# First chunk of a fused attention and feed-forward kernel: softmax sums from a column of ones in v, products scaled per row and transposed back, early buffers in place of late w_out weights

## The chip, the core and the metric

The kernel runs on one core of a Trainium2 chip. The core has a matrix engine (TensorE, PE in the profile; its loads of the stationary operand are PEld), three elementwise engines (VectorE or DVE, ScalarE or ACT, GpSimd or POOL), and a queue, SyncE or SP, that issues all transfers. Each engine works its own queue in order and waits on semaphores for the others. The metric is the device time of one execution in microseconds: the median of three runs was 625.05 us (624.15 to 625.32).

## What is computed

Attention over local windows and block summaries, then a two-layer feed-forward network. There are 4 batches, 8 heads, 768 positions, head size 64, model width 512 and hidden width 2048; all is float32.

```python
k_sum = k.reshape(B, H, nb, block, D).max(axis=3)      # 24 blocks of 32
v_sum = v.reshape(B, H, nb, block, D).mean(axis=3)
scores_l = scale * np.matmul(q, k.transpose(0, 1, 3, 2))
mask_l = np.abs(pos[:, None] - pos[None, :]) < window  # 16
scores_s = scale * np.einsum('bhsd,bhnd->bhsn', q, k_sum) + np.log(block)
scores_all = np.concatenate([np.where(mask_l, scores_l, -1e9), scores_s], axis=-1)
scores_all = scores_all - np.max(scores_all, axis=-1, keepdims=True)
a = np.exp(scores_all)
a = a / (np.sum(a, axis=-1, keepdims=True) + 1e-09)
x = np.matmul(a, np.concatenate([v, v_sum], axis=2))   # then tokens x 512
h = x @ w_in
return np.maximum(0.01 * h, h) @ w_out
```

## The kernel before

**Chunks and units.** The work is cut into 8 chunks (c) of 384 positions. Attention of a chunk runs in 12 units (u, UPC), one for each of four head pairs (p) and three tiles of 128 positions. A unit compares 64 queries at a time with 120 keys: 24 block maxima and 96 positions of a window. The output x of a unit is stored transposed (model width on the partitions) as a high part xh in the matrix engine's fp32r format and the rest xl, so that a product in float32 is three fp32r products. The feed-forward network takes a chunk through 16 hidden tiles (f): `m1` makes a hidden tile with 12 matmuls (L712), ScalarE and VectorE apply the leaky ramp and split it (L716, L719, L722), and `m2` adds its 9 products (L731 to L733) to three accumulators. Later chunks use a Strassen-like scheme (L899, L989), which the change does not touch.

**A unit of chunk 0** (`unit`, L389) goes through these steps, each an entry in the planner's list: `qk`, the scores (L359); `ttr`, mask and row minimum of the negated scores, one operation per head (`lowest`, L364); `ex`, the exponential with the row sum read from ScalarE's accumulator (`expo`, L371); `guard`, `rec` and `nrm`, which add 1e-9, invert the sum and multiply the exponentials by it (L408, L412, L416); `tr`, two transposes (L376); `pt`, a copy of these to SBUF (L427); `av`, four products with v as the stationary operand, which give x already transposed (L382); `xhi` (L433) and `xlo` (L436). Chunk 1 runs in pairs of units, chunks 2 to 7 in fours, between the feed-forward tiles of earlier chunks.

**What a unit needs.** The tile `k` holds q (loaded) and the keys of each tile of positions, copied from the k load `kn` by ScalarE (`windows`, L304, two per head pair) and from the block maxima `ksum` by VectorE (L237, L319). The tile `v` holds the v windows (loaded) and the block means. For batch 0 the means come from TensorE: `v_mean_pe` multiplies three loads `vb` with a small matrix (L273), ScalarE copies the result to `vs` (L278), and GpSimd spreads it into the four v tiles (L315). There are two buffers for k, three for v, two for pt and two for the exponentials e.

**Weights** come as 64-bit loads of 0.52 MB, one for each f and each of w_in (w = 0) and w_out (w = 1), into slots of `big`; VectorE, ScalarE, VectorE, ScalarE, VectorE (L668, L672, L675, L678, L681) turn each into a high and a low tile. The tiles of all 16 f of w_out, `wout_hi` and `wout_lo`, have their own space from the start.

**What sets the order.** A planner (`Plan`) takes all steps with an estimated cost, a priority and their dependences, and writes each engine's queue in the order in which it would run them. Priorities come from `PLACE` (the place of a unit in the stream, by chunk), `OFF` (a shift and a slope for each step of chunk 0 and 1) and a dozen constants (L50 to L64). `LOADS` fixes the order of the first transfers. The planner also decides how many matmuls on zeros (`spare`, L1092) TensorE runs where it expects nothing to do before the feed-forward part begins. What an engine really does at a time is in the trace alone.

## Time and profile before

| | |
|---|---|
| median of three runs | 625.05 us |
| the profiled execution | 625.08 us |
| its span in the trace | 623.3 us |
| TensorE busy | 616.4 us in 4496 matmuls |
| VectorE, ScalarE, GpSimd busy | 367.1, 321.5, 4.4 us |
| transfers | 102.16 MB, 164 GB/s over the span |
| granted clock of TensorE | 0.998 |

The span is the time from the first to the last recorded event; the execution is 1.8 us longer. In the rows that follow, L and a number is the line of the kernel, `out<-in` are the tiles, and the bracket at a row's end tells how long the engine had been idle before it and what ended that. In a table of stretches the columns are: start and end, length, then busy us and (in brackets) instructions of TensorE, its weight loads, VectorE, ScalarE and GpSimd, then the granted clock, the share of the transfer engines in use and GB/s. In a timeline they are start, duration, engine, line, operation and tiles. Matmuls overlap, so the distance from one start to the next tells more than a duration.

### The profile page before, as it was taken

The page shows a single profiled execution, that of the slowest core. Times are in us where ns is not written, and L with a number is a line of the kernel's source. Part 1 is how long each engine was busy: PE and PEld are TensorE (multiplying, and loading weights), DVE is VectorE, ACT ScalarE, POOL GpSimd, SP SyncE. Part 2 cuts the span into 40 slices and gives each one's busy share as a digit, 9 for nine tenths or more (in the row PEclk, how much of TensorE's full clock was granted, in tenths as well). Part 3 has the DMA queues.
Part 4 walks back from the last instruction along what each step waited for, and adds up shares of the span by engine and source line. Part 5 has one row for each costly group of instructions (what it writes and reads, how often), then busy time and mean ns, then how long its engine had stood idle before and what let it go on. Part 6 is the DMA issues. An engine that isn't in the chain of part 4 may idle for free.

```text
span 623.3 us, 12015 instructions
## 1 busy us (share of the span) xinstructions
PE 616.4 (99%) x4496; PEld 541.1 (87%) x4496; DVE 367.1 (59%) x1055; ACT 321.5 (52%) x914; POOL 4.4 (1%) x10
## 2 busy tenths in 40 slices
PE   9999999999999999999999999999999999999996
PEld 7687889888888888888898898989889898989895
DVE  5889999964899433445424763546446751535352
ACT  5889995644776255555525664535435351404040
POOL 0200000000000000000000000000000000000000
PEclk9999999999999999999999999999999999999999
DMA  8897996992787521374231471725416361616122
GB/s 284 249 298 243 291 289 202 367 306 93 227 270 245 144 75 51 90 222 111 83 113 52 124 238 56 221 84 149 124 60 195 118 202 36 202 35 202 38 66 101
DMA packets 58443, 102.16 MB, mean 164 GB/s; under 512 B 5584, under 2 KB 30224, under 8 KB 58384
## 3 DMA queue, kind: packets, MB, share of 16 engines
q1 hardware_dynamic: 58384, 101.38, 52.2%
q8 instruction: 36, 0.59, 0.4%
q14 instruction: 23, 0.19, 0.1%
HBM read 78.33 MB, written 20.97 MB: 159 GB/s over the span
## 4 chain that ended last, share of the span: by engine, by line
PE 94%; ACT 2%; DMA 2%; DVE 1%; issue 0%; DVEq 0%
PE L L989 21%; PE h L712 20%; PE a L731 7%; PE a L733 7%; PE a L732 7%; PE Z L899 5%; PE W L899 5%; PE X L899 5%; PE Y L899 3%; PE spare L1092 2%; DMA big<-in_w_dram 2%; PE vps L273 1%; ACT e L371 1%; PE s L359 0%; PE t L376 0%; ACT big L672 0%
## 5 line engine op out<-in xcount | busy, mean ns | idle before, releaser
L712 PE MATMUL h<-x,win_hi 128*128 128x384 f32 x512 | 131.8, 338 | 0.0
L712 PEld LDWEIGHTS h<-x,win_hi 128*128 128x128 f32 x512 | 92.7, 188 | 4.1
L712 PE MATMUL h<-x,win_lo 128*128 128x384 f32 x256 | 86.1, 336 | 0.0
L722 DVE TENSOR_TENSOR glo<-gs,ghi 128x384 fp32r<-128x384 f32 x64 | 35.5, 555 | 77.4 <-ACT gs L716 77.3
L731 PE MATMUL a<-wout_hi,ghi 128*128 128x512 f32 x192 | 77.4, 403 | 0.2 <-ACT wout_hi L678 0.2
L732 PE MATMUL a<-wout_lo,ghi 128*128 128x512 f32 x192 | 75.2, 392 | 0.5 <-DVE wout_lo L681 0.5
L733 PE MATMUL a<-wout_hi,glo 128*128 128x512 f32 x192 | 75.6, 394 | 0.0
L371 ACT ACTIVATE e<-e,m 128x120 f32<-128x120 f32 x192 | 73.5, 388 | 3.4 <-DVE m L364 3.2
L989 PE MATMUL L<-wout_hi,win_hi 128*128 128x512 f32 x192 | 75.2, 392 | 0.0
L989 PE MATMUL L<-wout_hi,win_lo 128*128 128x512 f32 x192 | 74.9, 390 | 0.0
L989 PE MATMUL L<-wout_lo,win_hi 128*128 128x512 f32 x192 | 74.8, 390 | 0.0
L719 ACT ACTIVATE ghi<-h 128x384 fp32r<-128x384 f32 x64 | 31.4, 491 | 82.9 <-PE h L712 82.4
L712 PEld LDWEIGHTS h<-x,win_lo 128*128 128x128 f32 x256 | 48.0, 188 | 0.0
L733 PEld LDWEIGHTS a<-wout_hi,glo 128*128 128x128 f32 x192 | 36.0, 188 | 8.5 <-DVE glo L722 0.4
L989 PEld LDWEIGHTS L<-wout_hi,win_lo 128*128 128x128 f32 x192 | 36.0, 188 | 7.7
L989 PEld LDWEIGHTS L<-wout_hi,win_hi 128*128 128x128 f32 x192 | 36.0, 188 | 7.0
L989 PEld LDWEIGHTS L<-wout_lo,win_hi 128*128 128x128 f32 x192 | 36.1, 188 | 7.0
L732 PEld LDWEIGHTS a<-wout_lo,ghi 128*128 128x128 f32 x192 | 36.1, 188 | 6.6 <-DVE wout_lo L681 1.2
L731 PEld LDWEIGHTS a<-wout_hi,ghi 128*128 128x128 f32 x192 | 36.1, 188 | 5.9 <-ACT wout_hi L678 0.5
L371 ACT ACTIVATION_READ_ACCUMULATOR e<-e,m 128x1 f32 x192 | 36.9, 192 | 0.0
L940 ACT ACTIVATE win_hi<-U 128x384 fp32r<-128x384 f32 x32 | 16.6, 518 | 38.8 <-DVE U L929 38.8
L955 ACT COPY P<-X 128x384 f32<-128x384 f32 x16 | 7.5, 470 | 50.8 <-PE X L899 49.5
(487 smaller groups left out, 1164.7 us busy)
## 6 DMA issues: line engine op xcount, KB each, us to landing
x<-sums SPq DMA_DIRECT2D x84, 256.0 KB
big<-in_w_dram SPq DMA_DIRECT2D x32, 512.0 KB
v<-in_v_dram SPq DMA_DIRECT2D x32, 288.0 KB
sums<-big SPq DMA_DIRECT2D x16, 512.0 KB
big<-in_k_dram SPq DMA_DIRECT2D x16, 400.0 KB
k<-in_q_dram SPq DMA_DIRECT2D x32, 192.0 KB
big<-in_vb_dram SPq DMA_DIRECT2D x12, 384.0 KB
win_hi<-sums SPq DMA_DIRECT2D x14, 256.0 KB
```

The costliest lines, as they stand in the source:

```text
L371: nc.scalar.activation(out=e[:, n], in_=e[:, n], func=AF.Exp, scale=-1.0, bias=m[:, n:n + 1], accum_out=z[:, n:n + 1])
L712: nc.tensor.matmul(h[:, :T], w[:, 512 * f + 128 * k:512 * f + 128 * k + 128], x[:, T * k:T * k + T], start=n == 0, stop=n == 11)
L719: nc.scalar.activation(out=gnew(tag, G("ghi", f)), in_=tl[G("h", f)][:, :T], func=AF.Prelu, alpha=0.01)
L722: nc.vector.tensor_tensor(out=gnew(tag, G("glo", f)), in0=tl[G("gs", f)], in1=tl[G("ghi", f)].bitcast(F32), op=ALU.subtract)
L731: nc.tensor.matmul(o, gh, wout_hi[:, f], start=f == f0, stop=False)
L732: nc.tensor.matmul(o, gh, wout_lo[:, f], start=False, stop=False)
L733: nc.tensor.matmul(o, gl, wout_hi[:, f], start=False, stop=f == f1 - 1)
L899: nc.tensor.matmul(o[:, :T], w[:, 256 * l + 128 * k:256 * l + 128 * k + 128], x[y][:, T * k:T * k + T], start=start and n == 0, stop=n == ...
L940: nc.scalar.activation(out=hi, in_=ps("X") if direct else tl[kt], func=AF.Prelu, alpha=0.01)
L955: nc.scalar.copy(tmp(K("P1")), ps("X"))
L989: nc.tensor.matmul(o, g, w[:, f], start=s + m == 0, stop=s == 1 and m == 5)
L1092: nc.tensor.matmul(spare[:, :128], zero[:, :128], zero[:, :128], start=True, stop=True)
```

## The change

For chunk 0 alone the exponentials are no longer normalised before they are transposed. The v tiles get 130 columns instead of 128: a column of ones ahead of the first head's and behind the second head's 64, loaded from a new input `v1`, and a further row of 1e-9 in those columns, against a row of ones in `pt`. The value product now has `pt` as the stationary operand and v with its column of ones as the moving one, so it gives 65 columns a head: x by rows, and the sum with its guard beside it. VectorE inverts the two sums (`rec`), scales x by rows (`scale`), TensorE transposes it back into the same bank (`back`), and `xhi` and `xlo` read that. The exponential no longer reads the accumulator, and the guard and the normalisation of e are gone. GpSimd fills the rows and columns of v and pt once at the start.

The last 6 of the 16 w_out tiles get buffers of their own (`late0`, `late1`). Until these are written, the same space (`attic`) holds further buffers of chunk 0: two more for k (q), one for v, four for pt, one for e, so that chunk 0 has four, four, six and three. The product's bank is chosen from two, or four after `HO`.

The planner's numbers change: its estimate of a transfer's latency and rate, some costs, `PLACE`, `OFF`, `LOADS`, and the constants, and the weights' steps are entered after the units.

```diff
-PLACE = {0: (0.0, 1.0), 1: (13.07, 0.61), 2: (22.42, 0.495), 3: (33, 0.8), 4: (43.2, 0.6), 5: (50.4, 0.7)}
+PLACE = {0: (0.015, 0.9806), 1: (13.192, 0.6413), 2: (22.504, 0.3532), 3: (32.642, 0.7357), 4: (43.127, 0.6174), 5: (50.638, 0.7154), 6: (59.023, 0.9778), 7: (71.251, 1.0473)}
...
-    LAT = {"SP": 910.0, "PE": 200.0, "DVE": 130.0, "ACT": 142.0, "POOL": 190.0,
+    LAT = {"SP": 60.0, "PE": 200.0, "DVE": 130.0, "ACT": 142.0, "POOL": 190.0,
...
-    def op(self, eng, cost, prio, fn, after=(), use=(), alloc=(), size=0, rate=250.0, port=False):
+    def op(self, eng, cost, prio, fn, after=(), use=(), alloc=(), size=0, rate=335.0, port=False):
...
-                dma = max(dma, end + 1200) + o["size"] / o["rate"]
+                dma = max(dma, end + 1500) + o["size"] / o["rate"]
...
+    attic = [cst.tile([128, (NF - SPL) * DM], F32, name=f"attic{n}", tag=f"late{n}") for n in range(2)]
...
+    room = {("k", 0, 2): (0, 0), ("k", 0, 3): (0, 1104), ("pt", 2): (0, 2208), ("v", 0, 3): (1, 0), ("pt", 3): (1, 784), ("pt", 4): (1, 1296), ("pt", 5): (1, 1808), ("e", 2): (1, 2320)}
...
+    for p in range(NP):
+        x = first_new("v", ("v", 0, p), [LK + 1, 2 * TPC, 130], VR)
+        nc.gpsimd.memset(x[96:], 0.0)
+        nc.gpsimd.memset(x[96:, :, 0:130:129], 1.0e-9)
+        nc.gpsimd.memset(x[:NS, :, 0:130:129], 1.0)
...
+            nc.gpsimd.memset(tl["pt", m][96:], 1.0)
...
-        def guard():
-            z = tiles_of(m)[2][:, part]
-            nc.vector.tensor_scalar(out=z, in0=z, scalar1=1e-9, scalar2=None, op0=ALU.add)
...
+        def soft(h):
+            e, x, _ = tiles_of(m)
+            n = 2 * (u % 2) + h
+            nc.scalar.activation(out=e[:, n], in_=e[:, n], func=AF.Exp, scale=-1.0, bias=x[:, n:n + 1])
...
         def av():
-            values(u, new(tag_o, ko, [128, 512], src=src_o, bufs=1), 0)
+            o = bank(ko)
+            for j in range(2):
+                for h in range(2):
+                    nc.tensor.matmul(o[64 * j:64 * j + 64, 65 * h:65 * h + 65], tl["pt", m][:, 2 * (u % 2) + h, 64 * j:64 * j + 64],
+                                     tl[kv][:, 2 * i + j, 65 * h:65 * h + 65], start=True, stop=True)
+
+        def rec():
+            nc.vector.reciprocal(out=new("rz", K("rz"), [128, 2]), in_=tl[ko][:, 0:130:129])
...
+        def back():
+            nc.tensor.transpose(out=tl[ko][:, 256:384], in_=tl[K("xr")], identity=ident)
 
         def xhi():
-            nc.scalar.copy(x_of(xh, c, r, 128), tl[ko][:, :128])
+            nc.scalar.copy(x_of(xh, c, r, 128), tl[ko][:, 256:384])
...
+        o = P.op("PE", 200, v + 2.05 + off("back"), back, after=[o], use=[ko, K("xr")])
...
-        o = P.op("ACT", ACT(512), t + 0.3, s4, after=[o], use=[kr])
+        o = P.op("ACT", ACT(512), t + 0.3, s4, after=[o] + ([x for k in room for x in P.users[k]] if w and f >= SPL else []), use=[kr])
...
+    P.settle("o", lambda t: ("a1", "to", "h0", "h1") if t > HO else ("a1", "to"))
```

**How the queues move.** SyncE's queue, from its first transfer, before (in_v_dram into big are the `vb` loads, 128x800 from in_k_dram the `kn` loads):

```order
L233 DMA big<-in_k_dram 128x800
L299 DMA k_1_101<-in_q_dram 128x384
L299 DMA k_0_103<-in_q_dram 128x384
L233 DMA big<-in_k_dram 128x800
L219 DMA mask<-in_mask_dram 128x404
L267 DMA big<-in_v_dram 128x1024
L233 DMA big<-in_k_dram 128x800
L267 DMA big<-in_v_dram 128x1024
L299 DMA k_2_232<-in_q_dram 128x384
L267 DMA big<-in_v_dram 128x1024
L233 DMA big<-in_k_dram 128x800
L660 DMA big<-in_w_dram 128x1024
```

And now, to the same weight load:

```order
L333 DMA k_0_125<-in_q_dram 128x384
L267 DMA big<-in_k_dram 128x800 x2
L333 DMA k_1_129<-in_q_dram 128x384
L253 DMA mask<-in_mask_dram 128x404
L301 DMA big<-in_v_dram 128x1024
L267 DMA big<-in_k_dram 128x800
L333 DMA attic_77<-in_q_dram 128x384
L301 DMA big<-in_v_dram 128x1024 x2
L344 DMA v_0_97<-in_v_dram 96x780
L267 DMA big<-in_k_dram 128x800
L333 DMA attic_77<-in_q_dram 128x384
L700 DMA big<-in_w_dram 128x1024
```

The third and fourth q loads go into space of their own (attic) and stand earlier, and the first v load stands ahead of the fourth kn load.

ScalarE's queue around the copy of the block means (`vs`) and around the twelfth x, before (L304 copies windows, L371 is the exponential, L427 pt, L433 x, L672 and L678 weights):

```order
L371 ACTIVATE e_355,z_357<-e_355,m_356 128x120 x4
L672 ACTIVATE big<-big 128x512
L278 COPY vs_398<-vps 24x512
L678 CAST win_hi<-big 128x512
L433 CAST x_80<-o_434 128x128
...
L433 CAST x_80<-o_639 128x128
L678 CAST wout_hi<-big 128x512
L433 CAST x_80<-o_663 128x128
L672 ACTIVATE big<-big 128x512
L371 ACTIVATE e_673,z_675<-e_673,m_674 128x120 x4
```

And now (L338 windows, L448 and L410 exponentials of chunk 0 and 1, L456 pt, L476 x, L712 weights):

```order
L448 ACTIVATE e_298<-e_298,m_299 128x120 x4
L456 COPY pt_114<-t_314 120x256
L338 COPY attic_77<-big 128x3x96 x2
L312 COPY vs_332<-vps 24x512
L456 COPY pt_114<-t_334 120x256
...
L712 ACTIVATE big<-big 128x512
L476 CAST x_82<-o_539 128x128
L476 CAST x_82<-o_546 128x128
L410 ACTIVATE e_535,z_537<-e_535,m_536 128x120 x2
L476 CAST x_82<-o_567 128x128
L712 ACTIVATE big<-big 128x512
L476 CAST x_82<-o_581 128x128
```

The windows of the fourth head pair stand right ahead of the copy of the means, and exponentials of chunk 1 (`m` 6) and two rescalings of weights stand among the last four x.

TensorE's queue where the feed-forward part begins (L712, now L752), before:

```order
L712 MATMUL h_0_618<-x_80,win_lo 128x384
L382 MATMUL o_639<-pt_631,v_3_467 64x64 x4
L376 MATMUL t_645<-ident,e_542 120x128 x2
L359 MATMUL s_('g', 6, 1)_649<-k_0_379 64x120 x2
L359 MATMUL s_('g', 6, 1)_650<-k_0_379 64x120 x2
L359 MATMUL s_('g', 6, 1)_649<-k_0_379 64x120 x2
L359 MATMUL s_('g', 6, 1)_650<-k_0_379 64x120 x2
L382 MATMUL o_663<-pt_631,v_3_467 64x64 x4
```

And now (L462 is the value product, L473 the transpose back):

```order
L415 MATMUL t_555<-ident,e_437 120x128 x2
L462 MATMUL o_567<-attic_78 64x65 x4
L473 MATMUL o_539<-ident,xr_564 128x128
L473 MATMUL o_546<-ident,xr_572 128x128
L462 MATMUL o_581<-attic_78 64x65 x4
...
L473 MATMUL o_567<-ident,xr_590 128x128
L473 MATMUL o_581<-ident,xr_600 128x128
L752 MATMUL h_0_608<-x_82,win_hi 128x384
L752 MATMUL h_0_608<-x_86,win_hi 128x384
L752 MATMUL h_0_608<-x_82,win_lo 128x384
```

Before, nine matmuls of the first hidden tile stood ahead of the last two value products and the scores of chunk 1; now all products and transposes of chunk 0 and these scores stand ahead of the first of them. Over the whole queue the spares fall from 164 to 53.

More of the change, by code (lines that the diff above doesn't have):

```diff
@@ L456, in unit @@
+        o2 = P.op("DVE", DVE(128), v + 2.2 + off("xlo"), xlo, after=[o1], use=[ko, ("x", c)])
         x_op.setdefault(c, []).extend([o1, o2])
@@ L987, in block @@
                         gh, gl = (y[:, 128 * i:128 * i + 128] for y in g_of(f, h))
[L988 to L989 removed]
+                        for g, w in ((gh, 0), (gh, 1), (gl, 0)):
+                            nc.tensor.matmul(o, g, wout(w, f), start=s + m == 0, stop=s == 1 and m == 5)
                             m += 1
@@ L1044, in build @@
         quad(q)
+    for f in range(NF):
+        for w in range(2):
+            weights(f, w, LEAD - WT + min(f, SPL) * WS + max(f - SPL, 0) * WS2 + WO * w + (W0 if f == 0 else 0))
     t = LEAD
```

161 lines of the change are left out of this document (86 added, 75 removed).

## Prediction

> **What bounds the kernel now.** I read the page's busy shares first, then the table by stretches, then the timeline of the first 35 us, engine by engine.
>
> ```profile
> PE 616.4 (99%) x4496; PEld 541.1 (87%) x4496; DVE 367.1 (59%) x1055; ACT 321.5 (52%) x914; POOL 4.4 (1%) x10
> ...
> 34.59:60.00 25.41, 24.67 (x193) 20.64 (x191) 23.25 (x77) 22.92 (x67) 0.00 (x0) 1.00 0.87 269
> 60.00:80.00 20.00, 20.00 (x170) 17.16 (x169) 19.73 (x58) 19.04 (x50) 0.00 (x0) 1.00 0.94 288
> ...
> 500.00:623.30 123.30, 118.29 (x592) 106.58 (x590) 49.81 (x89) 33.94 (x74) 0.00 (x0) 0.99 0.35 109
> ```
>
> The columns after the stretch are its length, then busy us of PE, PEld, DVE, ACT, POOL, then clock, DMA share and GB/s. From 34.59 us on TensorE loses 0.74 us before 60, nothing in the next row, and 5.0 us in the last, which is the way out. So the span is (the moment at which the dense part starts) + (a fixed amount of TensorE work). Before that moment "busy" deceives, since part of it is matmuls on zeros (spare, L1092):
>
> ```profile
> 0.99 6.35 PE L1092 MATMUL spare<-zero 128*128 128x128 bf16 x61 [0.99 <-DVE zero L1084]
> 7.84 1.40 PE L1092 MATMUL spare<-zero 128*128 128x128 bf16 x22
> ...
> 22.18 0.69 PE L382 MATMUL o<-pt,v 120*64 120x64 f32 x16
> ...
> 30.39 0.60 PE L712 MATMUL h<-x,win_hi 128*128 128x384 f32 x2
> ...
> 33.83 0.95 PE L1092 MATMUL spare<-zero 128*128 128x128 bf16 x14
> 34.59 0.64 PE L712 MATMUL h<-x,win_hi 128*128 128x384 f32 x2
> ```
>
> The first two of the twelve value products (L382) run at 22.18. Nine of the first feed-forward tile's twelve matmuls slip in at 30.39, the other three and everything behind them start at 34.59. What sets that is ScalarE:
>
> ```profile
> 20.56 0.57 ACT L278 COPY vs<-vps 24x512 f32<-24x512 f32 x1 [1.57 <-PE vps L273]
> 21.05 0.66 ACT L678 CAST win_hi<-big 128x512 fp32r<-128x512 f32 x1
> 22.68 0.27 ACT L433 CAST x<-o 128x128 fp32r<-128x128 f32 x1 [0.98 <-PE o L382]
> ...
> 33.56 0.69 ACT L678 CAST wout_hi<-big 128x512 fp32r<-128x512 f32 x1
> 34.13 0.28 ACT L433 CAST x<-o 128x128 fp32r<-128x128 f32 x1
> 34.28 0.70 ACT L672 ACTIVATE big<-big 128x512 f32<-128x512 f32 x1
> 34.86 0.40 ACT L371 ACTIVATE e<-e,m 128x120 f32<-128x120 f32 x1
> ```
>
> No value product can run before the block means of v are copied out (L278, 20.56); the twelfth x (L433) is issued at 34.13 and passes at 34.28. Between them lie 13.72 us in which ScalarE idles 0.98 us in one piece. **So two numbers decide: when L278 starts, and how long ScalarE's queue is from there to the twelfth x.**
>
> **When L278 starts.** DMA feeds everything ahead of it:
>
> ```profile
> 0.00:2.00 2.00, 1.01 (x10) 1.02 (x11) 0.11 (x1) 1.27 (x1) 0.70 (x6) 1.00 0.21 32
> 2.00:10.00 8.00, 8.00 (x109) 7.34 (x107) 3.62 (x17) 3.20 (x14) 0.00 (x0) 1.00 0.94 348
> 10.00:12.00 2.00, 2.00 (x12) 0.33 (x10) 1.97 (x15) 1.59 (x8) 0.00 (x0) 1.00 0.63 162
> 12.00:16.00 4.00, 3.87 (x53) 2.79 (x53) 2.39 (x13) 2.92 (x11) 0.00 (x0) 1.00 0.91 349
> 16.00:22.00 6.00, 6.00 (x49) 2.49 (x47) 5.02 (x24) 4.08 (x16) 0.80 (x2) 1.00 1.04 268
> 22.00:26.00 4.00, 3.98 (x75) 2.87 (x72) 3.11 (x18) 3.30 (x14) 2.87 (x4) 1.00 0.37 106
> 26.00:34.59 8.59, 8.57 (x128) 6.67 (x127) 7.52 (x34) 8.35 (x32) 0.00 (x0) 1.00 0.99 313
> ...
> 7.07 0.77 ACT L304 COPY k<-big 128x288 f32<-128x288 f32 x2 [2.35 <-DMA big<-in_k_dram]
> ```
>
> There are holes at 10 to 12 and 22 to 26, where SyncE's queue stood behind a load whose buffer was taken. With four buffers for q and four for v those waits go. On ScalarE the changed program puts the windows of the fourth head pair ahead of L278's copy, and these need kn 3 and q 3, the 12th and 13th loads, 4.50 MB into the stream (tile sizes added up in the new order). Moved by 10 us: 0.06 + 8 x 0.348 = 2.85 MB; at 349 GB/s after it, 4.50 MB is reached at 14.7. A load can land later than its bytes are due: kn 1, 1.21 MB into the old stream, was waited for until 7.07, when 0.06 + 5.07 x 0.348 = 1.83 MB had moved. That lag of 0.62 MB gives 5.12 MB, of which 4.94 MB is there at 16 and the rest, at 268 GB/s, at 16.7. I take the middle, 15.7, add the pair of windows, and let L278 start at 16.4 (15.4 to 17.4). **It moves up by 4.2 us.**
>
> **How long ScalarE's queue is.** Pitches, start to start:
>
> ```profile
> 10.36 0.38 ACT L371 ACTIVATE e<-e,m 128x120 f32<-128x120 f32 x1
> 10.65 0.18 ACT L371 ACTIVATION_READ_ACCUMULATOR e<-e,m 128x1 f32 x1
> 10.74 0.38 ACT L371 ACTIVATE e<-e,m 128x120 f32<-128x120 f32 x1
> ...
> 14.58 0.77 ACT L304 COPY k<-big 128x288 f32<-128x288 f32 x2
> 15.25 0.37 ACT L427 COPY pt<-t 120x256 f32<-120x256 f32 x1
> 15.51 0.40 ACT L371 ACTIVATE e<-e,m 128x120 f32<-128x120 f32 x1
> ```
>
> An exponential costs 0.38 with its read of the sum and 0.29 without, a window 0.335, a copy of pt 0.26; from the rows above, L278 0.49, a cast of weights 0.57, x 0.15, a rescaling of weights (L672) 0.58. Counted off before's order from L278 to the twelfth x: 0.49, 3 casts 1.71, 12 x 1.80, 8 pt 2.08, 4 windows 1.34, 8 exponentials 3.04, 2 rescalings 1.16: 11.62 us, so 2.10 of the 13.72 are gaps. The same piece of the changed program: 0.49, 2 casts 1.14, 12 x 1.80, 9 pt 2.34, 4 windows 1.34, 8 exponentials without the read 2.32, 3 of chunk 1 with it 1.14, 4 rescalings 2.32: 12.89 us. **The queue does not get shorter:** the dropped reads save 0.72 here, but two rescalings and three exponentials of chunk 1 that stood behind the twelfth x now stand ahead of it. With the same gaps it takes 14.99 and ends at 31.4. Gaps of 1.1 (without the one-piece wait) would give 30.4, one more us of gaps 32.4.
>
> **The new steps.** VectorE loses twelve guards and has twelve normalisations half as wide; nearest rows:
>
> ```profile
> L416 DVE TENSOR_TENSOR e<-e,z 128x240 f32<-128x240 f32 x12 | 4.7, 402 | 0.1
> L436 DVE TENSOR_TENSOR x<-o,x 128x128 fp32r<-128x128 f32 x12 | 3.5, 290 | 0.9 <-ACT x L433 0.8
> L408 DVE TENSOR_SCALAR z<-z 128x2 f32<-128x2 f32 x12 | 2.0, 165 | 2.1 <-ACT e L371 2.1
> L412 DVE RECIPROCAL z<-z 128x2 f32<-128x2 f32 x12 | 1.9, 159 | 0.1
> ...
> 23.78 0.38 PE t L376 x2
> ...
> 58.49 2.11 PE h L712 x12
> ```
>
> That is 12 x (165 + 402 - 290) = 3.3 us less on VectorE, which is off the chain (the rows by stretch add up to 23.7 us of work in the first 34.59), so I count nothing; were it the chain, 3.3 us would be the gain. Per unit, reciprocal 0.16, scaling 0.29 and a transpose (half of 0.38) now stand between product and x: 0.64 us of latency, where guard, reciprocal and normalisation (0.73) stood ahead of the transpose of e. They overlap between units; if the last unit shows its own, it costs 0.6. The twelve transposes are 12 x 0.19 = 2.3 us of TensorE, in time that spares filled; a 65-wide product beside a 64-wide one is nothing. All twelve transposes stand ahead of the first feed-forward matmul in TensorE's queue, so the nine matmuls that before ran at 30.39 in the shadow no longer do. They need units 0 to 8 alone, and the last transpose out of their way; between those and the twelfth x ScalarE has two exponentials, a rescaling and two x, 2 x 0.38 + 0.58 + 2 x 0.15 = 1.6 us, as long as the nine themselves (9/12 of the last row). So they can just hide. Before, the dense part came 0.31 us after the twelfth x had passed (34.59 - 34.28), which gives 31.7; I add 0.4 for what of the nine sticks out and let the three last ones start at 32.1.
>
> GpSimd gets 18 memsets. Nearest row:
>
> ```profile
> 0.73 0.20 POOL masks.py:197 MEMSET ident<- 128x128 f32 x1 [0.29 <-POOLq L1136]
> ```
>
> By elements, four of 780 cost 1.2 us each, six of 512 0.8, eight small ones at most 0.2: all are done by 13, the v tiles' first, before kn 3 can land. I take nothing; late, they cost up to 1 us. The late w_out tiles wait for the early buffers' last readers: the first comes 21 MB into the stream, where 9.7 MB have moved by 32.1 (below), so this wait costs nothing. The other shifts of order (chunks 1 to 7) can win at most the 0.74 us that TensorE loses; I take nothing, bounds -0.7 and +1.5.
>
> **Sum.** 34.59 - 32.1 = 2.5 us off the span. The profiled execution took 625.08 us around its span of 623.3, at the runs' median of 625.05. 625.08 - 2.5 = **622.6 us**.
>
> **Rivals.**
> *Weights come late, and the gain is given back: 625.*
>
> ```profile
> 36.01 10.49 DMA big<-in_w_dram
> ...
> PE a L732 <- DVE wout_lo L681: 0.5, 1, 0.5
> ```
>
> A transfer of weights leads the chain right behind the start already. In the new stream the first w_out tile ends at 9.94 MB instead of 7.58, since two w_in tiles and another w_out tile were put ahead of it. With no hole, 2.85 + 6 x 0.349 + 6 x 0.268 + 10.1 x 0.313 = 9.7 MB have moved by 32.1, so it lands at 33 to 35 (the lag above); rescaling, joining and two casts, four steps of 0.6, make it 35.4 to 37.4. TensorE asks for it after three matmuls and two tiles of twelve, at 32.1 + 0.5 + 2.1 + 2.1 = 36.8, plus a burst of chunk 1's scores. So it lies between 1.4 us early and 0.6 late. For this rival: so little room. Against: by bytes the stream is ahead (9.7 MB at 32.1, 9.3 at 34.59 before). If one tile slips by another lag (2 us) and the next by a little, the 2.5 are gone.
>
> *The clock falls, slower than before: 627.* The 61 spares above ran at 104 ns, the 22 behind them at 64: TensorE's speed rises once it has been kept busy. The changed program has 53 spares instead of 164, and between the last block of v (3.60 MB) and the fourth pair's operands lie 0.9 MB, 2.6 us of stream, in which it may wait idle. From the first value product, at 16.4 + (22.18 - 20.56) = 18.0, to the feed-forward it has 12 products of 0.35, 7 pairs of 0.38 and 12 transposes of 0.19: 9.1 us in 14. At half speed these are 18.2, with scores on top; the dense part starts at 36.2 or later, 1.6 us after before's: 625.08 + 1.6 = 626.7. It decides if the drop comes before 18 and holds; such gaps did not occur before, so the trace is silent.
> The Trainium skill, "TensorE: Matmul & The Clock Gate", Part 1, says the clock drops after an idle window of about 3.4 us; by that rule a wait of 2.6 us does not reach it, and 622.6 stands. No run here shows it yet.
>
> *The queue gets shorter than I count: 619.8.* If L278 starts at 15.4, gaps are 1.1 and the nine matmuls hide, the dense part starts at 15.4 + 12.89 + 1.1 + 0.3 = 29.7, 4.9 us early, and 0.3 of the stalls stay away.
>
> **How the numbers follow.** Forecast (621.0 to 623.7) 0.52; shorter queue (below 621) 0.16; weights late (623.8 to 626.2) 0.20; clock or a stall of that size (above 626.3) 0.12. Runs of this kernel tell 0.2% (1.25 us) from nothing: faster is below 623.8, slower above 626.3, which gives 0.68, 0.20 and 0.12. The range leaves out the far ends of the first and last: 620.0 to 625.8.
>
> **What would show it.** L278's line 4 us earlier, at 15.4 to 17.4, right behind the fourth pair of windows; the twelfth x at 31 to 32; no hole in DMA before 30; the first dense matmul at 30 to 32; the same 0.7 us of stalls before 60. It is wrong if spares or matmuls before 30 run at double pitch, if TensorE waits over 1 us for w_out, or if a wait for reciprocal or scaling, not ScalarE's queue, leads into the twelfth x.

## Result and profile after

| | before | after |
|---|---|---|
| median | 624.6 us (623.8 to 625.3, 4 runs) | 634.5 us (630.35 to 634.97, 4 runs) |
| ratio | | 1.0144, 95% interval 1.0099 to 1.0189 |
| the profiled execution, its span | 625.08, 623.3 us | 630.35, 627.9 us |

The change makes the kernel slower by 1.4%. The profiled execution is the fastest of the four after; the other three, of which there is no trace, are 4.1 to 4.6 us longer. Eight executions of 675 us or more, four of kernels below and four of the kernel before, are left out of every median and range here.

The page and the table by stretches of the changed kernel, with the columns as before; the first row starts where the tenth matmul of the first feed-forward tile does (33.87, before 34.59):

```profile
PE 614.0 (98%) x4397; PEld 537.0 (86%) x4397; DVE 366.4 (58%) x1043; ACT 319.9 (51%) x890; POOL 11.1 (2%) x28
...
33.87:60.00 26.13, 25.65 (x199) 22.30 (x199) 24.48 (x75) 23.81 (x62) 0.00 (x0) 1.00 0.78 243
60.00:80.00 20.00, 18.21 (x139) 15.67 (x137) 19.11 (x57) 17.62 (x48) 0.00 (x0) 0.91 0.89 286
80.00:130.00 50.00, 46.50 (x316) 40.84 (x316) 44.82 (x109) 31.87 (x80) 0.00 (x0) 1.00 0.82 268
130.00:500.00 370.00, 369.73 (x2809) 327.64 (x2808) 199.48 (x598) 185.04 (x551) 0.00 (x0) 1.00 0.45 139
500.00:627.90 127.90, 124.04 (x624) 112.23 (x622) 55.64 (x98) 36.96 (x78) 0.00 (x0) 1.00 0.37 116
```

Two rows of the kernel before, which the first parts don't show:

```profile
80.00:130.00 50.00, 50.00 (x295) 44.77 (x293) 47.46 (x101) 32.51 (x75) 0.00 (x0) 1.00 0.90 293
130.00:500.00 370.00, 370.00 (x2840) 328.49 (x2840) 203.09 (x619) 188.37 (x560) 0.00 (x0) 1.00 0.46 141
```

Length minus TensorE's busy time is what it loses: 0.48, 1.79, 3.50, 0.27, and 3.86 on the way out. Up to 500 us that is 6.04, where it was 0.74 before; the way out is 1.15 shorter. So the dense part (from that tenth matmul to the end of the span) starts 0.72 earlier, then takes 594.0 instead of 588.7 us, and the span grows by 4.6. Of the 5.3 us that the dense part grew, idle time gives +5.30, the way out -1.15, a cut of the clock (0.91 in the second row, below) +1.7 if it is counted as lost time; -0.5 is left over.

The waits of TensorE from 40 to 130 us (who waited, for whom, us in total, times, longest):

```profile
PE to_('g', 10, 1)_985 L415 <- DVE e L553: 1.8, 1, 1.8
PE s_('g', 13, 1)_1244 L421 <- DVE x L570: 1.5, 1, 1.5
PE s_('A', 6)_1518 L398 <- ACT gs L756: 1.4, 1, 1.4
PE to_('B', 6)_1626 L415 <- DVE z L658: 0.6, 1, 0.6
PE to_('g', 9, 1)_877 L415 <- DVE e L553: 0.5, 1, 0.5
```

None of them is a wait of TensorE for weights. The first is for a normalisation of chunk 1 (L553, nrm). Its place in VectorE's timeline, then the transposes in TensorE's:

```profile
61.73 0.18 DVE L549 RECIPROCAL z<-z 128x4 f32<-128x4 f32 x1
62.55 0.43 DVE L708 TENSOR_SCALAR big<-big 128x512 int32<-128x512 int32 x1 [0.64 <-DMA big<-in_w_dram]
62.90 0.65 DVE L553 TENSOR_TENSOR e<-e,z 128x480 f32<-128x480 f32 x1
...
63.69 0.62 PE L415 MATMUL to_('g', 10, 1)_985<-ident,e 128*120 128x128 f32 x4 [1.79 <-DVE e L553]
```

The normalisation needs nothing from DMA: its reciprocal was there at 61.9. But in VectorE's queue the first step on a tile of weights (L708, s0) stands ahead of it, and that tile lands at 62.5. TensorE has nothing else in front and waits. In the kernel before, a weight step stood ahead of a normalisation in the same way, but its tile was there, and VectorE went straight on:

```profile
61.57 0.40 DVE L668 TENSOR_SCALAR big<-big 128x512 int32<-128x512 int32 x1
61.89 0.66 DVE L510 TENSOR_TENSOR e<-e,z 128x480 f32<-128x480 f32 x1
```

Ahead of the second wait ScalarE's copy pt of a pair (L560, 83.16) stood behind three weight steps (from 81.29 on), although the transposes that it copies had started at 80.66. For the third the table names a ramp step of ScalarE (L756) that was done at 112.1. What came last, by VectorE's timeline, is its copy of block maxima into k (L356, 112.58 to 112.81), behind a maximum that had waited 1.1 us for its k load (L271, 110.58) and a step on weights (L871).

Behind the first wait the clock is cut to a half, by the rows for single microseconds:

```profile
62.00:63.00 1.00, 0.00 (x0) 0.00 (x0) 0.45 (x2) 1.00 (x3) 0.00 (x0) 1.00 1.01 263
63.00:64.00 1.00, 0.31 (x3) 0.34 (x4) 1.00 (x3) 0.87 (x2) 0.00 (x0) 1.00 0.95 324
64.00:65.00 1.00, 1.00 (x7) 1.00 (x6) 1.00 (x3) 0.07 (x1) 0.00 (x0) 0.73 1.00 384
65.00:66.00 1.00, 1.00 (x5) 1.00 (x4) 1.00 (x3) 0.78 (x2) 0.00 (x0) 0.50 0.71 161
66.00:67.00 1.00, 1.00 (x4) 1.00 (x4) 1.00 (x5) 1.00 (x3) 0.00 (x0) 0.50 1.00 381
67.00:68.00 1.00, 1.00 (x4) 0.99 (x4) 0.84 (x6) 1.00 (x7) 0.00 (x0) 0.56 0.98 369
```

0.27 + 0.50 + 0.50 + 0.44 = 1.71 us are lost at half speed. In the first chunk, ScalarE's and TensorE's timelines read:

```profile
17.48 0.57 ACT L312 COPY vs<-vps 24x512 f32<-24x512 f32 x1
32.73 0.28 ACT L476 CAST x<-o 128x128 fp32r<-128x128 f32 x1
32.88 0.42 ACT L410 ACTIVATE e<-e,m 128x120 f32<-128x120 f32 x1
...
31.93 0.33 PE L473 MATMUL o<-ident,xr 128*128 128x128 f32 x1 [0.26 <-DVE xr L469]
32.22 0.59 PE L752 MATMUL h<-x,win_hi 128*128 128x384 f32 x2
...
33.87 0.51 PE L752 MATMUL h<-x,win_hi 128*128 128x384 f32 x2
```

The copy of the block means comes 3.1 us earlier (17.48), the twelfth x passes at 32.88 instead of 34.28, and nine matmuls now stand between the last transpose back and the tenth.

### The profile page after: what moved, and what is told of

Read it like the earlier page. It is cut to its first block, busy times and chain, and to the rows that moved or that the text cites. A ratio compares the mean times of both kernels' runs of the same rounds, so it can differ in the third digit from the quotient of the medians.

```text
span 627.9 us, 11805 instructions
## 1 busy us (share of the span) xinstructions
PE 614.0 (98%) x4397; PEld 537.0 (86%) x4397; DVE 366.4 (58%) x1043; ACT 319.9 (51%) x890; POOL 11.1 (2%) x28
## 4 chain that ended last, share of the span: by engine, by line
PE 78%; DMA 10%; DVE 7%; ACT 2%; issue 1%; SPq 0%; ACTq 0%; DVEq 0%
PE L L1029 21%; PE h L752 15%; DMA big<-in_w_dram 8%; PE Z L939 5%; PE X L939 5%; PE W L939 5%; PE a L773 5%; PE a L771 5%; PE a L772 5%; PE Y L939 3%; DMA big<-in_vb_dram 1%; DVE glo L762 1%; DVE big L715 1%; DMA big<-in_k_dram 1%; ACT big L712 1%
## 5 line engine op out<-in xcount | busy, mean ns | idle before, releaser
L752 PE MATMUL h<-x,win_hi 128*128 128x384 f32 x512 | 132.8, 340 | 0.0
L752 PEld LDWEIGHTS h<-x,win_hi 128*128 128x128 f32 x512 | 93.3, 189 | 4.2
L752 PE MATMUL h<-x,win_lo 128*128 128x384 f32 x256 | 86.9, 339 | 0.0
L410 ACT ACTIVATE e<-e,m 128x120 f32<-128x120 f32 x168 | 64.3, 388 | 5.9 <-DVE m L403 5.9
L759 ACT ACTIVATE ghi<-h 128x384 fp32r<-128x384 f32 x64 | 31.3, 489 | 70.2 <-PE h L752 70.1
L752 PEld LDWEIGHTS h<-x,win_lo 128*128 128x128 f32 x256 | 48.5, 189 | 0.2 <-DVE win_lo L721 0.2
L771 PE MATMUL a<-wout_hi,ghi 128*128 128x512 f32 x120 | 48.4, 404 | 0.0
L773 PE MATMUL a<-wout_hi,glo 128*128 128x512 f32 x120 | 47.3, 394 | 0.0
L1029 PE MATMUL L<-wout_hi,win_hi 128*128 128x512 f32 x120 | 47.0, 391 | 0.0
L772 PE MATMUL a<-wout_lo,ghi 128*128 128x512 f32 x120 | 46.9, 391 | 0.0
L1029 PE MATMUL L<-wout_hi,win_lo 128*128 128x512 f32 x120 | 46.8, 390 | 0.0
L1029 PE MATMUL L<-wout_lo,win_hi 128*128 128x512 f32 x120 | 46.7, 389 | 0.0
L1029 PE MATMUL L<-wout,win_hi 128*128 128x512 f32 x144 | 44.6, 391 | 0.0
L410 ACT ACTIVATION_READ_ACCUMULATOR e<-e,m 128x1 f32 x168 | 32.2, 192 | 0.0
L756 ACT ACTIVATE gs<-h 128x384 f32<-128x384 f32 x64 | 31.0, 485 | 0.0
L771 PE MATMUL a<-wout,ghi 128*128 128x512 f32 x72 | 28.8, 400 | 0.0
L939 PE MATMUL X<-win_hi,x 128*128 128x384 f32 x96 | 28.6, 338 | 0.0
```

What stands on the lines that cost most here:

```text
L410: nc.scalar.activation(out=e[:, n], in_=e[:, n], func=AF.Exp, scale=-1.0, bias=m[:, n:n + 1], accum_out=z[:, n:n + 1])
L752: nc.tensor.matmul(h[:, :T], w[:, 512 * f + 128 * k:512 * f + 128 * k + 128], x[:, T * k:T * k + T], start=n == 0, stop=n == 11)
L756: nc.scalar.activation(out=new("gs", G("gs", f), [128, T], bufs=1), in_=tl[G("h", f)][:, :T], func=AF.Prelu, alpha=0.01)
L759: nc.scalar.activation(out=gnew(tag, G("ghi", f)), in_=tl[G("h", f)][:, :T], func=AF.Prelu, alpha=0.01)
L771: nc.tensor.matmul(o, gh, wout(0, f), start=f == f0, stop=False)
L772: nc.tensor.matmul(o, gh, wout(1, f), start=False, stop=False)
```

## Experiments

Theories. **T1**: the planner's new model of the transfers (60 ns after landing for 910, 335 bytes/ns for all transfers instead of 250 and 290, a delay of 1500 ns for 1200) plans weights earlier than they land, so their steps stand ahead of attention steps in VectorE's and ScalarE's in-order queues. **T2**: the new placement numbers of chunks 1 to 7. **T3**: the first chunk's rewrite itself. **T4**: cuts of the clock behind waits. Two came up on the way: **T5**, the order of the first two loads, and **T6**, T1's mechanism inside the first chunk.

All times, each with the ratio to the runs of the kernel before on the same chip (its medians were 624.0 to 624.6).

| kernel | median us (range) | ratio, 95% interval |
|---|---|---|
| again: after, unchanged | 632.3 (629.9 to 633.4) | 1.0133 (1.0095 to 1.0171) |
| model: old transfer model | 626.1 (625.6 to 627.3) | 1.0036 (1.0024 to 1.0048) |
| tables: old placement numbers | 635.3 (632.8 to 636.6) | 1.0178 (1.0146 to 1.0211) |
| both: the two together | 629.5 (627.6 to 630.0) | 1.0082 (1.0054 to 1.0111) |
| w290: old weights' rate alone | 628.5 (626.3 to 629.0) | 1.0064 (1.0046 to 1.0083) |
| before_model: before, new model | 638.3 (636.6 to 639.8) | 1.0233 (1.0214 to 1.0252) |
| hybrid: new model up to 16 us | 626.9 (624.1 to 630.0) | 1.0043 (1.0022 to 1.0064) |
| fill: spares ahead of two waits | 632.4 (630.1 to 633.5) | 1.0129 (1.0111 to 1.0148) |
| kfirst: after, k loaded first | 631.8 (630.3 to 634.7) | 1.0131 (1.0101 to 1.0161) |
| hybrid_k: hybrid, k loaded first | 627.1 (624.7 to 631.0) | 1.0042 (1.0021 to 1.0064) |
| before_q: before, q loaded first | 623.8 (622.8 to 624.8) | 0.9993 (0.9982 to 1.0004) |
| after_s0: after, VectorE's first weight step later | 631.2 (630.0 to 633.5) | 1.0121 (1.0101 to 1.0141) |
| after_s02: ScalarE's first weight step later too | 633.4 (632.8 to 635.2) | 1.0157 (1.0143 to 1.0172) |
| late_s0: mixed model, k first, VectorE's step later | 625.8 (624.8 to 628.2) | 1.0028 (1.0015 to 1.0041) |
| late_s0_fill: the same with 32 spares | 626.3 (624.4 to 628.6) | 1.0037 (1.0024 to 1.0050) |
| late_s02: late_s0 with ScalarE's step later too | 624.7 (623.0 to 627.4) | 1.0017 (1.0002 to 1.0033) |
| late_s02_fill: the same with 32 spares | 625.5 (623.8 to 628.2) | 1.0029 (1.0016 to 1.0043) |

### Which part of the change costs the time

*again*, the changed kernel once more.

> The changed kernel as it is, for a profile of another execution and its spread. T1 (weight steps that wait for their DMA stand ahead of attention steps in VectorE's queue, TensorE waits, and its clock is cut after the longer waits): the same PE waits at pairs 9 to 13, 5 to 7 us of idle time between 32 and 125 us; an execution of 632 us has either more granted-clock loss or longer waits than the 6.0 us of the one profiled. If the extra 4 us of three of the four executions lie elsewhere (start, tail), T1 explains only half.

Its profile has the same two waits as the longest (2.6 and 1.7 us), 5.9 us of idle time between the tenth matmul and 500 us and one cut of the clock, as T1 had said.

*model*, the old transfer model in the changed kernel:

```diff
-    LAT = {"SP": 60.0, "PE": 200.0, "DVE": 130.0, "ACT": 142.0, "POOL": 190.0,
+    LAT = {"SP": 910.0, "PE": 200.0, "DVE": 130.0, "ACT": 142.0, "POOL": 190.0,
...
-    def op(self, eng, cost, prio, fn, after=(), use=(), alloc=(), size=0, rate=335.0, port=False):
+    def op(self, eng, cost, prio, fn, after=(), use=(), alloc=(), size=0, rate=250.0, port=False):
...
-                dma = max(dma, end + 1500) + o["size"] / o["rate"]
+                dma = max(dma, end + 1200) + o["size"] / o["rate"]
...
-        o = load_op(("w", f, w), t - 0.25 * BIG, load, alloc=[("big", kr, 0)], size=128 * 4096, rate=335.0)
+        o = load_op(("w", f, w), t - 0.25 * BIG, load, alloc=[("big", kr, 0)], size=128 * 4096, rate=290.0)
```

> Only the planner's model of the transfers is put back (latency 910 after an issue, 250 bytes/ns and 290 for weights, 1200 ns); the new placement numbers and the whole new first chunk stay. T1: the weight steps ahead of pair 9's normalisation ask for 14.9 MB of the stream instead of 17.0, of pair 10's for 16.8 instead of 19.0, so the PE waits of 1.8 and 1.5 us go to under 0.7 in sum and the time falls to 621 to 625. T2 (the new placement numbers of chunks 1 to 7 cost the time, whatever the model): stays at 629 or more. T3 (the first chunk's rewrite itself): stays at 629 or more.

*tables* puts back `PLACE` of chunks 1 to 7, `PL`, `WS`, `WS2`, `LD`, `XP`, `B1`, `B2`, `WT`, `W0` and `WO`, and keeps the new model:

```diff
-PLACE = {0: (0.015, 0.9806), 1: (13.192, 0.6413), 2: (22.504, 0.3532), 3: (32.642, 0.7357), 4: (43.127, 0.6174), 5: (50.638, 0.7154), 6: (59.023, 0.9778), 7: (71.251, 1.0473)}
+PLACE = {0: (0.015, 0.9806), 1: (13.07, 0.61), 2: (22.42, 0.495), 3: (33, 0.8), 4: (43.2, 0.6), 5: (50.4, 0.7)}
...
```

> Only the placement numbers of chunks 1 to 7 and of the weights are put back; the new transfer model and first chunk stay. T1: pair 10's normalisation still stands behind weights that need 18.5 MB of the stream, after 24.3 us of TensorE's work instead of 28.2: waits as long or longer, 629 to 636. T2: 622 to 626. T3: 629 or more.

*both* is the two diffs together.

> Transfer model and later placement numbers both put back; what is left of the change is the first chunk's new structure with its own numbers and the early buffers in place of late weights. T1 and T2: 622 to 625, about 0.8 us of gain at the start against the kernel before, no PE wait over 0.7 us between 32 and 125 us. T3: 629 or more, and the loss would then be sought in the first chunk and its buffers.

TensorE's waits in *model*:

```profile
PE spare L1133 <- DVE zero L1125: 1.0, 1, 1.0
PE h L752 <- ACT win_hi L718: 0.7, 1, 0.7
PE h L752 <- DVE win_lo L721: 0.5, 2, 0.3
PE to_('B', 6)_1735 L415 <- DVE z L654: 0.3, 1, 0.3
```

The four numbers of the model are worth 632.3 - 626.1 = 6.2 us, three quarters of the loss, and behind the start no wait over 0.7 us is left. T3, which had asked for 629 or more, falls as the main cause. The old placement numbers don't help with either model (635.3 against 632.3, 629.5 against 626.1): T2 falls. *both* came out 4.5 us above what T1 had said, where T3 had put it. Its profile shows the loss ahead of the dense part: the tenth matmul comes at 37.98, 2.8 us later than in *model*, and the dense part is about as long (589.5 and 589.0). The likely reason is that the old numbers don't fit the new first chunk; T1's wording there was too wide.

Why the model does it is seen by setting the start that the planner gives to a step beside the start in the trace. For the first weight step (L708) of each load, in the order of VectorE's queue, the planner's own list against the profiled execution, us:

| step | after: planned | traced | model: planned | traced |
|---|---|---|---|---|
| 1st | 17.4 | 19.2 | 22.6 | 22.3 |
| 5th | 31.1 | 34.3 | 40.1 | 40.2 |
| 12th | 49.8 | 54.8 | 57.7 | 58.1 |
| 18th | 62.3 | 68.7 | 70.1 | 70.7 |
| 32nd | 90.8 | 99.9 | 99.8 | 102.0 |

With 335 bytes/ns the plan runs 1.8 us ahead of the chip at the first weight and 9.1 at the last. With the old numbers it is within 0.6 us up to the 18th. The chip moved 243 to 286 GB/s from 34 to 130 us (rows above). This is not all that its transfer engines could do: their share in use was 0.78 to 0.89, and SyncE's weight loads waited 39 us there for slots of `big` that weight steps had still to free. How much of the drift is the rate and how much these waits, no run separates. The queues were worked in order, so every attention step behind a weight step that was planned too early inherits the error.

*w290* puts back the weights' rate alone, *before_model* gives the model to the kernel before:

```diff
-        o = load_op(("w", f, w), t - 0.25 * BIG, load, alloc=[("big", kr, 0)], size=128 * 4096, rate=335.0)
+        o = load_op(("w", f, w), t - 0.25 * BIG, load, alloc=[("big", kr, 0)], size=128 * 4096, rate=290.0)
```

> Of the changed kernel's planner model one number is put back: the rate at which w_in and w_out are planned to arrive, 290 bytes/ns instead of 335. T1 (the planned rate): pair 9's normalisation stands behind weights up to 16.0 MB of the stream instead of 17.0, pair 10's behind 17.9 instead of 19.0, so about two thirds of the way to the kernel with the whole old model: waits of TensorE between 40 and 130 us under 2 us in sum (6.0 in the changed kernel), 623 to 627. If the loss came of the model's delays (60 for 910 ns, 1500 for 1200), which stay: 630 or more.

> The kernel before with the new transfer model alone (latency 60, 335 bytes/ns for all, 1500 ns). T1: it is slowed as the changed kernel is, pair 10's normalisation stands behind 17.9 MB after 25.4 us of TensorE's work (17.3 MB after 29.8 without the model): 628 to 634, with waits of TensorE for VectorE's normalisations between 45 and 125 us. T3 (the rewrite of the first chunk is what made the stream late): 624 to 626.

TensorE's longest waits in *before_model* (line numbers of the kernel before):

```profile
PE s_('A', 6)_1527 L359 <- issue: 1.9, 1, 1.9
PE to_('g', 12, 1)_1212 L376 <- DVE e L510: 1.7, 1, 1.7
PE vps L273 <- DMA big<-in_v_dram: 1.3, 1, 1.3
PE h L712 <- ACT gs L716: 1.3, 1, 1.3
PE s_('g', 13, 1)_1255 L382 <- DVE x L527: 1.2, 1, 1.2
```

The model alone, with nothing of the rewrite, costs the kernel before 14 us, even more than T1 had said, and the transposes of a pair wait for a normalisation (L510) again. More than half of that lies in the first chunk: the tenth matmul comes at 42.5 instead of 34.6, with the clock cut for 10 us, and the dense part takes 595.5 us instead of 588.7. One rate gives back 3.8 of the 6.2 us, a little less than the two thirds that were expected, and leaves 3.0 us of idle time from 40 to 130 us where under 2 had been said. Its tenth matmul comes late, at 37.55, and its dense part of 589.7 us is nearly as short as in *model*.

The dense part sorts all profiles by the model that plans it. It takes 593.0 to 595.5 us in the eight kernels with the new model throughout (after, *again*, *tables*, *before_model*, *fill*, *kfirst*, *after_s0*, *after_s02*) and 587.1 to 589.7 in the eleven with the old weights' rate or the old or a slower model behind the first chunk, whatever their first chunk is like. So T1 is shown there from both sides, at 4 to 7 us. The rest of each time is decided by when the dense part starts, from 33.3 us (*late_s02*) to 42.5 (*before_model*).

### The clock

*fill* keeps TensorE busy at the two longest waits:

```diff
+        def fill(t, n):
+            for _ in range(n):
+                nc.tensor.matmul(t[:, :128], zero, zero, start=True, stop=True)
+
         def tr():
+            fill(tl["to", gt], 28 if gt == ("g", 10, 1) else 0)
...
             def run(x=groups[g], g=g):
+                if g == ("g", 13, 1):
+                    t = new("to", ("fill", g), [128, 512], src=ps_t, bufs=1)
+                    for _ in range(28):
+                        nc.tensor.matmul(t[:, :128], zero, zero, start=True, stop=True)
```

> The changed kernel with 28 spare 128x128 bfloat16 matmuls in TensorE's queue ahead of the transposes of pair 9 (bank of the transposes) and 28 ahead of pair 11's products (in the same bank), the two places where it waits 1.5 to 2.6 us; nothing else moves. T4 (the granted clock is cut after such a wait, and that costs another 1.5 to 2 us each time): no stretch under 0.95 behind these two places, the same lateness of the normalisations, and the time falls by 1.5 to 3 us, to 629 to 631, and spreads less. If the cuts are not caused by the waits, or cost nothing: 632 to 634 as before.

The two filled places show no cut. But the third wait, which the table puts down to ScalarE (L765, the line of `gs` in this kernel), grew from 1.4 to 2.1 us. Again VectorE's copy of block maxima came last, at 114.57, behind a k load that came 2.0 us later than in after. The clock was cut there instead (another cut stands at 9.0, behind a wait of 1.9 us in the first chunk):

```profile
113.00:114.00 1.00, 0.00 (x0) 0.00 (x0) 1.00 (x2) 1.00 (x4) 0.00 (x0) 1.00 0.94 294
114.00:115.00 1.00, 0.10 (x4) 0.13 (x8) 1.00 (x3) 0.10 (x1) 0.00 (x0) 0.92 0.90 309
115.00:116.00 1.00, 1.00 (x9) 0.70 (x10) 0.94 (x1) 0.00 (x0) 0.00 (x0) 0.50 1.02 291
116.00:117.00 1.00, 1.00 (x4) 0.71 (x4) 0.00 (x1) 0.00 (x0) 0.00 (x0) 0.50 1.03 348
117.00:118.00 1.00, 1.00 (x4) 0.81 (x3) 1.00 (x1) 0.00 (x0) 0.00 (x0) 0.50 1.07 380
118.00:119.00 1.00, 1.00 (x6) 0.78 (x5) 1.00 (x10) 0.56 (x3) 0.00 (x0) 0.87 1.10 399
```

The time did not move (632.4, where T4 had said 629 to 631). A cause for that which fits, but which no run isolates: the work that waits on the stream of loads cannot be won by speeding TensorE up ahead of it. So T4 holds as far as cuts come behind waits; that they cost time beyond the waits is read from the windows, 1.7 us each, and not shown by the times. Two profiles speak against it: *after_s0* and *kfirst* have no cut in the dense part before the way out, and it takes 594.1 and 593.2 us, against 594.0 and 594.1 in after and *again* with one cut each.

### What the first chunk's rewrite is worth

*hybrid* separates the two ends: the new model for what is issued early, the old one behind it, so that the first chunk keeps the changed kernel's order.

```diff
-            free[e] = end
+            free[e], late = end, t > 16000
...
-                dma = max(dma, end + 1500) + o["size"] / o["rate"]
+                dma = max(dma, end + (1200 if late else 1500)) + o["size"] / ((290 if o["rate"] > 335 else 250) if late else 335)
...
-                x["ready"] = max(x["ready"], end + self.LAT.get((e, x["eng"]), self.LAT[e]) if x in o["next"] else free[e])
+                x["ready"] = max(x["ready"], end + (850 if late and e == "SP" else 0) + self.LAT.get((e, x["eng"]), self.LAT[e]) if x in o["next"] else free[e])
```

(The weights' rate is 336 there, to tell them apart.)

> The changed kernel, with its own transfer model for what is issued before 16 us of the plan and the old one (1200 ns, 250 and 290 bytes/ns, 910 after landing) behind it. The first chunk's order is the changed kernel's up to the last rows of it, the later one asks for as little of the stream as the kernel with the old model. T1: start of the changed kernel (block means' copy at 17.5 us, first m1 at 32 to 32.5), no wait over 0.7 us behind it: TensorE's work left at 40 us (576.3 us in the changed kernel) plus 1.4 of idle time and a tail of 3.9 gives a span of 621.5 and a time of 622.5 to 624.5, a little under the kernel before. If the first chunk's rewrite itself costs time: 625.5 or more.

The late waits are gone in its profile, and its dense part (588.1 us) is as short as before's. But its executions fall between 624 and 630, where 622.5 to 624.5 had been said. In the changed kernel q of the first head pair is issued ahead of k; *kfirst* and *hybrid_k* swap the two, and *before_q* puts a q load ahead of the first k in the kernel before:

```diff
-LOADS = [('q', 0, 0), ('kn', 0, 0), ('kn', 0, 1), ('q', 0, 1), ...
+LOADS = [('kn', 0, 0), ('q', 0, 0), ('kn', 0, 1), ('q', 0, 1), ...
```

> The changed kernel with its first two loads swapped, so that k of the first pair of heads goes ahead of q as in the kernel before; no other instruction changes its place. T5 (k issued second shares its transfer with two others and lands 0.3 to 2.3 us later and at varying times, and TensorE's wait for it of up to 2.8 us cuts the clock in some executions): the first maximum over k starts at 3.7 to 4.2 us instead of 4.3 to 5.3, TensorE's idle time before 10 us falls to 1.0 to 1.5 us (2.2 and 2.4), the block means' copy comes at 17 us, and the time falls by 0.5 to 2 us, to 630 to 632, with the late waits as before. If the order of these two loads does not matter: 632 to 634.5.

> The kernel with the first chunk's own transfer model and the old one behind 16 us, and the first two loads swapped. T1 and T5 together: the slower of its executions (626 to 630 with the loads as changed) go, none with a clock cut before 20 us, 622.5 to 624.5. If the spread from 624 to 630 has another cause, the median stays at 626 to 628.

> The kernel before with q of the second pair of heads issued ahead of k of the first; no other instruction moves. T5: the first maximum over k starts 0.5 to 2 us later (3.95 in the kernel before), TensorE's start with it, 624.5 to 627 and a wider spread. If the order does not matter: 623.5 to 624.5.

T5 falls: k does come earlier in *kfirst* (first maximum over it at 3.75 us, 4.29 in after) and 631.8 lies just inside what T5 had said, but none of the three differs measurably from the kernel that it is made of. The two profiles show instead two things that can lengthen an execution, a cut of the clock inside the first chunk and a wait of VectorE for the first tile of weights. The clock in *kfirst* (every third row), and the first weight step of VectorE in *hybrid_k*:

```profile
24.00:25.00 1.00, 1.00 (x16) 0.77 (x16) 0.52 (x4) 0.37 (x1) 0.00 (x0) 0.50 1.02 402
...
27.00:28.00 1.00, 1.00 (x14) 0.68 (x14) 0.67 (x5) 0.96 (x5) 0.00 (x0) 0.50 0.95 287
...
30.00:31.00 1.00, 1.00 (x19) 0.71 (x19) 0.76 (x2) 0.87 (x3) 0.00 (x0) 0.82 1.05 321
```

```profile
22.58 0.61 DVE L708 TENSOR_SCALAR big<-big 128x512 int32<-128x512 int32 x1 [2.02 <-DMA big<-in_w_dram]
```

VectorE's step on the first tile of weights, planned for 17.4, starts between 19.2 and 23.1 in the profiles of after, *again*, *tables*, *hybrid*, *hybrid_k* and *kfirst*, with the first chunk's last score steps behind it in the queue. VectorE waited 2.0 us for the tile in *hybrid_k*, 1.8 in *tables*, 0.7 in *kfirst*, 0.2 in after, and not at all in *again* and *hybrid*. So the mechanism of T1 sits inside the first chunk too, in some executions (T6). The edits that move the two first steps of this tile:

```diff
         o = P.op("DVE", DVE(512, True), t + 0.05, s0, after=[o0], use=[kr])
+        if f + w == 0:
+            o["behind"] = scale_op[2]
         o2 = P.op("ACT", ACT(512), t + 0.07, s2, after=[o0], use=[kr])
+        if f + w == 0:
+            o2["behind"] = pt_op[7]
```

`scale_op` and `pt_op` hold the first chunk's scaling steps and copies pt by unit. The kernels s0 have the first edge, s02 both; *late* kernels stand on *hybrid_k* with the switch at 14 us and 235 and 270 bytes/ns behind it; the two kernels whose names end in fill add 32 spares in the first chunk.

> The changed kernel with one edge more in its planner: VectorE's first step on the first weight (s0) stands behind the scaling of the first chunk's third tile instead of ahead of the first chunk's last score steps. The first weight lands between 18.9 and 22.5 us in the runs so far, and the later steps stand behind it. T6 (this one weight, landing late in some executions, holds the first chunk's last softmax steps, TensorE goes idle and its clock is cut for 7 to 9 us): no cut between 20 and 34 us, and the slower half of the changed kernel's executions (633 to 635) goes: 629 to 632 with a spread under 2 us, the late waits as before. If the spread comes of the late waits alone: 630 to 635 as before.

> All that has been found together: the changed kernel with its transfer model up to 14 us of the plan and a slower one behind it (1200 ns, 235 bytes/ns, 270 for weights, 910 after landing), k of the first pair loaded first, the first weight's s0 behind the third tile's scaling. T1 and T6: the slow half of the executions of the two kernels with a mixed model (626 to 631) goes, none with a cut between 20 and 34 us; 623 to 625. Without T6: 624 to 630 with a median of 627.

> As late_s0, with 32 spare bfloat16 matmuls more in TensorE's queue: 8 ahead of the first tile's scores, 12 ahead of the third's, 6 ahead of each of the first two transposes back, the places where it is idle 0.4 to 2 us. T4: no execution with a cut in the first 12 us either; 622.5 to 624.5 and a spread under 1.5 us. If cuts there cost nothing: as late_s0.

> As late_s0, with the first weight's first ScalarE step (s2) behind the eighth tile's copy of the transposed weights as well: in late_s0 that step waited 1.8 us for the weight's DMA and held the copy pt, and TensorE, in the execution with the cut. T6: no cut between 20 and 34 us in any execution, 623 to 625 with a spread under 1.5 us. If 625.5 to 626 again, ScalarE's step was not the cause of the median.

> late_s02 with the 32 spare matmuls of late_s0_fill. If cuts remain that come of TensorE's idle time in the first 9 us: 0.5 to 1 us under late_s02; else the same within 0.3 us.

> The changed kernel with the first weight's s0 and s2 both behind the first chunk's last softmax steps and nothing else. T6: 629 to 631, no execution over 632; the late waits of the transfer model stay (5 to 7 us of idle time from 40 to 130 us). If executions at 633 to 635 remain, the cuts behind the late waits make the spread, not the first chunk.

With VectorE's step moved, ScalarE's waited in its place (*late_s0*, first row); with both moved in the changed kernel, the next tile of weights did the same 9 us later, and TensorE stood still for the copy behind it (*after_s02*, the other rows):

```profile
20.86 0.66 ACT L712 ACTIVATE big<-big 128x512 f32<-128x512 f32 x1 [1.81 <-DMA big<-in_w_dram]
```

```profile
30.19 0.68 ACT L712 ACTIVATE big<-big 128x512 f32<-128x512 f32 x1 [2.47 <-DMA big<-in_w_dram]
...
31.73 0.62 PE L415 MATMUL t<-ident,e 128*120 128x128 f32 x2 [2.65 <-ACT attic L456]
```

*late_s02* is the best: its profiled execution, the fastest of its twelve, took 623.0 us, with the copy of the block means at 17.10 and the tenth matmul at 33.28:

```profile
17.10 0.57 ACT L312 COPY vs<-vps 24x512 f32<-24x512 f32 x1
31.79 0.35 ACT L476 CAST x<-o 128x128 fp32r<-128x128 f32 x1
...
33.28 0.51 PE L756 MATMUL h<-x,win_hi 128*128 128x384 f32 x2
```

Its median is 624.7, still not under the kernel before. The spares changed nothing that can be measured. T6's waits and cuts are in the traces, but its numbers mostly failed. *after_s0* has no cut in the first chunk and 631.2 us, not clear of *again*, with a spread of 3.4 us where 2 had been said; *late_s0* has a cut at 23 us and 625.8, above its range; *late_s02* lies in its range, with a spread of 4.4 us where 1.5 had been said; *after_s02* lies above its range, with cuts at 8, 32 and 90 us. Moving one tile's steps did not end the spread. What makes some executions of *late_s02* 2 to 4 us longer than others stays open; no version here beats both kernels.

## Why the prediction was wrong

The forecast was 622.6 us, faster; the kernel is slower.

- **The step that failed** is "The other shifts of order (chunks 1 to 7) can win at most the 0.74 us that TensorE loses; I take nothing, bounds -0.7 and +1.5." They cost 5.3 us of idle time in the profiled execution; the clock was cut by 1.7 us besides, a price that the times don't show. The new transfer model was treated as a detail of the planner, though it decides how far ahead weight steps stand in two in-order queues; *model* and *before_model* show that it is worth 6 us here and 14 in the kernel before, where over half of it falls in the first chunk.
- **Rival "weights come late, and the gain is given back"** had the right cause, but looked for it at TensorE (a wait for w_out). The lateness of loads reached TensorE through the queues of VectorE and ScalarE, first by a normalisation that needs no weights, and cost 5.3 us and the cut where the rival gave 2.5.
- **Rival "the clock falls"** came true in kind, but at 64.5 us, where the rival had placed it before 18. In four relatives of the changed kernel (*tables*, *hybrid_k*, *kfirst*, *late_s0*) a cut fell nearer to that, inside the first chunk, between 23 and 33 us. By the rule of the Trainium skill ("TensorE: Matmul & The Clock Gate", Part 1: cold after an idle window of about 3.4 us), a wait of 1.79 us would not have done it; the trace says it can.
- **Rival "the queue gets shorter than I count"** did not come: with 12.89 us of steps the gaps were 2.51 us, not 1.1. (Its sum gives 619.9, where it says 619.8.)
- **When L312 starts**: forecast 16.4 (15.4 to 17.4), measured 17.48, and 18.41 in *again*. TensorE, not the landing of kn 3, came last there: the copy pt ahead of the windows waited 0.39 us for transposes, and from it to L312 ScalarE had no idle time.
- **How long ScalarE's queue is**: forecast 14.99, measured 15.40 (32.88 - 17.48). Right: as said, it does not get shorter.
- **The nine matmuls** "can just hide": they run from 32.22 to 33.87, and 0.66 of their 1.65 us lie ahead of the twelfth x. The dense part came 0.99 us behind that x, where 0.3 and 0.4 had been allowed.
- So the gain at the start was 0.72 us instead of 2.5: 1.1 was lost at L312, 0.4 in the queue, 0.3 behind the twelfth x. In the last two the mechanism was right and the size was off; in the first kn 3 had been named and TensorE came last.
- **The new steps** cost nothing on GpSimd, and TensorE waits for no late w_out tile. The scaling does show: the last transpose back waited 0.26 us for it (row at 31.93), and the transposes back 1.1 us in all. Under *late_s02* the start came near the forecast (17.10, twelfth x at 31.79, tenth matmul 1.3 us earlier than before) in an execution of 623.0; its median shows that as a rule nothing is gained.
- **The signs of being wrong** that the prediction named did not come: no double pitch before 30 us, no wait of over 1 us for w_out, no wait for reciprocal or scaling that leads into the twelfth x. All of them watched the start, and the loss came behind 60 us.

The profiled execution lies 7.8 us above the forecast of 622.6 and the median 11.9; what the three longer executions lost besides is in no trace. Of the loss of 8.2 us in the runs of *again*, the transfer model is 6.2. For the other 2 us (*model* against before) the two profiles show 0.9 us: the tenth matmul comes at 35.14, 0.55 later than before. That the first chunk's numbers were set for the new model would fit, but is not shown. How much of it is the rewrite's own stays open.

## What to carry to other kernels

A planner's constants are part of the program: when a change touches a rate or a latency by which queues are ordered, compare planned with traced start times of the same steps, and price the drift, before looking at what the change is named after. In an in-order queue a step that waits for a transfer should stand behind the work that doesn't need that transfer: here planning with 335 bytes/ns instead of 250 and 290 (and the delays) cost 6 us. And when a wait is found, look at the row ahead of the releaser on the releaser's own engine, not only at the releaser.
